# An attention and mixture-of-experts kernel: where the pieces of the product with the values stand among the nine steps of a pair

## The chip, the cores and the metric

The kernel runs on one core of a Trainium2 chip. The metric is the device time in microseconds (us) of one launch, as the median of three runs. The core's engines are called as the profile calls them: PE (TensorE, the matrix products; PEld is its loading of the stationary operand), DVE (VectorE), ACT (ScalarE), POOL (GpSimd) and SP (SyncE, which here only issues DMAs).

## The reference, cut to what matters

Eight batches of eight heads, 576 tokens, 64 values per head. Rotary embedding of q and k, softmax attention, then a mixture of eight experts with one expert for each token:

```python
q_rot, k_rot = rotate(q), rotate(k)
scores = scale * np.matmul(q_rot, k_rot.transpose(0, 1, 3, 2))
scores = scores - np.max(scores, axis=-1, keepdims=True)
attn = np.exp(scores)
attn = attn / (np.sum(attn, axis=-1, keepdims=True) + 1e-09)
x = np.matmul(attn, v)                 # 4608 tokens x 512
e_idx = np.argmax(x @ w_gate, axis=1)
...
h = np.maximum(x[mask] @ w1[e], 0.0)
out[mask] = gate_w * eom * (h @ w2[e])
```

The change touches the attention part alone.

## The kernel before, in words

Attention runs over 32 pairs (8 batches, 4 pairs of heads each). The scores of a pair are made in nine steps, numbered 0 to 8. A step makes 128 rows of scores for one head: steps 0 and 1 are the first 128 queries for head 0 and head 1, steps 2 and 3 the next 128, steps 5 and 6, and 7 and 8 likewise. Step 4 is the remainder of 64 queries for both heads at once. `Attention.step` issues, for each step in this order:

- `scores` (L473 in step 4, L480 in the others): six matrix products on PE into one of two score buffers (`ps_s`, two of them). Head 0 uses partitions 0 to 63 of its operands, head 1 uses 64 to 127, step 4 uses all 128.
- `peak` (L486): DVE takes the row maxima of the scores.
- `exp` (L495): ACT takes the exponential, which reads the score buffer for the last time. So the scores of step i+2 can't begin before the exponential of step i is over.
- events placed at this step with order 0 or 1,
- `turn` (L501): DVE turns the exponentials of the step before in 32x32 blocks,
- events with order 2 or 3.

All engines run their instructions in the order in which they were issued. What else is done in a step is listed in `EVENTS`, as (name, steps after the pair's first step, order). An offset from 9 to 17 falls into steps 0 to 8 of the next pair. The product with the values (`values`, L523) is made of 18 blocks of 32 keys. A block is eight matrix products with 32 partitions each, which the profile counts as 16 instructions. The blocks are issued in four pieces, av0 to av3, while the scores of the next pair are being made. Then follow, in order: `evict` (ACT copies the result out, L530 to L532, offset 17), `back` (PE turns it and multiplies it with the gates, L541, offset 19, that is step 1), and `divide` (DVE divides by the sums of the exponentials, L548 to L556, also step 1). The result of the next pair's pieces lies in the same PSUM tile `acc`, so av0 can't begin before `divide` of the pair before is over.

Other work of a pair that the text speaks of: ACT and POOL split the next pair's keys and queries in two parts (`kh`, `qh` at L403, `kl`, `ql` at L411), POOL multiplies and adds for the rotary embedding (L429, L433), DVE takes reciprocals of the sums (`den1`, L507), ACT moves one column (`den2`, L510).

After the fourth pair of a batch, `place` sorts the batch's tokens by expert. Its parts are spread over the following pairs, at `PLACE` (20) plus an offset, counted in steps from that fourth pair. Five of its parts (`ones`, L702, on DVE) stand at `ROWS`; five others (`places`, L709, on POOL) stand at `PLACES`. One part is a PE product (`s14`, L673 and L674, with the DVE operations L678 and L679 behind it, which need `base`, L661, from POOL) in step 1, and another is `s20` (L717, PE, with L720 on DVE behind it), also in step 1. So the pairs come in four kinds, which follow one another and are called by these parts below: the three-`ones` pair, the two-`ones` pair, the `s20` pair and the `s14` pair. The first three-`ones` pair is pair 8 (pairs are counted from 0), the last is pair 28. The second to last batch has its `ones` elsewhere.

The mixture of experts follows attention and is made of the same engines; it uses none of what is changed.

Of the kernel before, what the change touches and what calls it, by code (L numbers as in the profile page):

```python
# [44 lines left out]
EVENTS = [  # L45
# [3 lines left out]
    ("den0", 10, 2), ("den1", 12, 2), ("den2", 13, 2), ("evict", 17, 2), ("newxb", 18, 1), ("back", 19, 1), ("divide", 19, 2),  # L49
]  # L50

# [4 lines left out]
}  # L56

PIECES = ((0, 5), (5, 10), (10, 14), (14, 18))
PLACE, PM = 20, 3
LISTED = 44  # L60
ROWS, PLACES = (28, 30, 32, 37, 39), (25, 29, 31, 34, 38)

TURN = 1

# [178 lines left out]
class Attention:  # L243


    def __init__(self, tc, nb, pools, cc, ident, ii, first, trib, oneb, cnt, zero, qk, v, xd, row, lists):
# [34 lines left out]
        for n, pr in enumerate(self.pairs):  # L281
# [5 lines left out]
            for t in range(2):  # L287
# [3 lines left out]
                fs[f"loadv{t}"] = lambda pr=pr, t=t: pr.loadv(t)  # L291
            for k, (b0, b1) in enumerate(PIECES):
                fs[f"av{k}"] = lambda pr=pr, b0=b0, b1=b1: [pr.values(j) for j in range(b0, b1)]
# [950 lines left out]
```

## Time and profile before

| | |
|---|---|
| median of three runs | 1053.69 us (1051.94 to 1054.26) |
| time of the profiled execution | 1050.29 us |
| its span | 1048.4 us (the rest, 1.9 us, lies around it) |
| PE busy | 1002.2 us, 96% of the span |
| DVE busy | 819.4 us, 78% |
| ACT busy | 628.6 us, 60% |
| POOL busy | 599.5 us, 57% |
| granted PE clock, mean | 0.993 |

The profile counts a matrix product as busy from its start to its modelled end, and products overlap in it, so a PE that is shown busy may still be waiting. Where a stretch is looked at, the starts of the instructions tell more than the busy share does. The timeline view merges successive instructions of one engine, line and kind into one row, with the start, the time until the last one's end and, behind x, the count.

### The profile page before, as it was taken

The page shows a single profiled execution, that of the slowest core. Times are in us where ns is not written, and L with a number is a line of the kernel's source. Part 1 is how long each engine was busy: PE and PEld are TensorE (multiplying, and loading weights), DVE is VectorE, ACT ScalarE, POOL GpSimd, SP SyncE. Part 2 cuts the span into 40 slices and gives each one's busy share as a digit, 9 for nine tenths or more (in the row PEclk, how much of TensorE's full clock was granted, in tenths as well). Part 3 has the DMA queues.
Part 4 walks back from the last instruction along what each step waited for, and adds up shares of the span by engine and source line. Part 5 has one row for each costly group of instructions (what it writes and reads, how often), then busy time and mean ns, then how long its engine had stood idle before and what let it go on. Part 6 is the DMA issues. An engine that isn't in the chain of part 4 may idle for free.

```text
span 1048.4 us, 34822 instructions
## 1 busy us (share of the span) xinstructions
PE 1002.2 (96%) x14461; PEld 872.3 (83%) x14461; DVE 819.4 (78%) x1371; ACT 628.6 (60%) x1283; POOL 599.5 (57%) x613
## 2 busy tenths in 40 slices
PE   5999999999999999998889999999999999999995
PEld 4888888888888888887778899998889888899984
DVE  6788889898888988888777867667777867857772
ACT  4566666666666666665545444556765765857762
POOL 4777888897988879888740121305343443443621
PEclk9999999999999999999999999999999999999998
DMA  6654665565645657465457966666986977987860
GB/s 217 179 149 131 183 182 140 161 172 172 191 131 173 190 142 205 119 184 135 111 188 280 298 229 194 210 218 234 332 285 221 350 242 270 324 293 253 291 248 28
DMA packets 58209, 216.32 MB, mean 206 GB/s; under 512 B 9351, under 2 KB 9660, under 8 KB 53952
## 3 DMA queue, kind: packets, MB, share of 16 engines
q1 hardware_dynamic: 50304, 194.03, 59.4%
q0 software_dynamic: 6464, 18.92, 5.0%
q8 instruction: 115, 1.88, 0.8%
q10 hardware_dynamic: 1280, 1.11, 0.3%
q14 instruction: 46, 0.38, 0.1%
HBM read 196.04 MB, written 20.09 MB: 206 GB/s over the span
## 4 chain that ended last, share of the span: by engine, by line
PE 66%; DVE 13%; issue 7%; ACT 7%; POOL 5%; DMA 1%; ACTq 0%; POOLq 0%; DVEq 0%
PE py L1120 17%; PE ph L1078 14%; PE sc L480 13%; PE acc L523 11%; ACT pm L495 4%; PE ph L1070 4%; DVE m L486 4%; POOL raw L429 3%; DVE pt L501 2%; DVE wl L1037 2%; PE acc L541 2%; PE mtp L1043 1%; ACT kh L403 1%; ACT wh L1035 1%; DVE xb L548 1%
## 5 line engine op out<-in xcount | busy, mean ns | idle before, releaser
L495 ACT ACTIVATE pm<-sc,m 128x576 f32<-128x576 f32 x288 | 213.3, 741 | 202.7 <-DVE m L486 201.3
L1037 DVE TENSOR_TENSOR wl<-wr,wh 128x1024 fp32r<-128x1024 f32 x184 | 252.6, 1386 | 44.8 <-ACT wh L1035 42.5
L486 DVE TENSOR_REDUCE m<-sc 128x1 f32<-128x576 f32 x288 | 212.8, 739 | 67.0 <-PE sc L480 60.4
L480 PE MATMUL sc<-kh,q 64*128 64x288 f32 x1024 | 222.2, 325 | 20.3 <-ACT q L403 9.9
L501 DVE STREAM_TRANSPOSE pt<-pm 128x576 f32<-128x576 f32 x288 | 219.5, 762 | 0.3 <-ACT pm L495 0.3
L1120 PE MATMUL py<-wh,ht 128*128 128x512 f32 x640 | 215.4, 401 | 0.0
L1035 ACT CAST wh<-wr 128x1024 fp32r<-128x1024 f32 x208 | 212.6, 1050 | 0.0
L523 PE MATMUL acc<-pt,v 32*64 32x128 f32 (+1 forms) x9216 | 198.1, 296 | 9.5 <-issue 4.8
L480 PEld LDWEIGHTS sc<-kh,q 64*128 64x128 f32 x1024 | 147.2, 191 | 62.3 <-ACT pm L495 28.6
L523 PEld LDWEIGHTS acc<-pt,v 32*64 32x64 f32 x9216 | 158.4, 131 | 33.8 <-issue 25.9
L429 POOL TENSOR_TENSOR raw<-raw,rt 128x1152 f32<-128x1152 f32 x62 | 164.1, 2646 | 0.3
L1078 PE MATMUL ph<-xt,wh 128*128 128x256 f32 x896 | 161.1, 282 | 0.5 <-DVE xt L1059 0.5
L1120 PEld LDWEIGHTS py<-wh,ht 128*128 128x128 f32 x640 | 120.2, 188 | 25.7
L1078 PEld LDWEIGHTS ph<-xt,wh 128*128 128x128 f32 x896 | 138.3, 188 | 2.4 <-DVE xt L1059 1.3
L1078 PE MATMUL ph<-xt,wl 128*128 128x256 f32 x448 | 126.1, 281 | 0.0
L1120 PE MATMUL py<-wl,ht 128*128 128x512 f32 x320 | 125.9, 394 | 0.0
L480 PE MATMUL sc<-kl,q 64*128 64x288 f32 x512 | 110.6, 297 | 0.8 <-issue 0.8
L1037 POOL TENSOR_TENSOR wl<-wr,wh 128x1024 fp32r<-128x1024 f32 x24 | 58.4, 2432 | 90.2 <-ACT wh L1035 83.8
L433 POOL TENSOR_TENSOR raw<-raw 128x576 f32<-128x576 f32 x62 | 87.5, 1411 | 1.9
L1094 ACT ACTIVATE ht<-ph 128x512 fp32r<-128x512 f32 x56 | 33.4, 597 | 90.6 <-PE ph L1078 90.6
L480 PEld LDWEIGHTS sc<-kl,q 64*128 64x128 f32 x512 | 84.0, 191 | 1.1 <-issue 1.0
L1078 PEld LDWEIGHTS ph<-xt,wl 128*128 128x128 f32 x448 | 84.4, 188 | 0.1
(247 smaller groups left out, 1304.3 us busy)
## 6 DMA issues: line engine op xcount, KB each, us to landing
wr<-in_w SPq DMA_DIRECT2D x208, 512.0 KB
raw<-in_qk SPq DMA_DIRECT2D x64, 576.0 KB
v<-in_v SPq DMA_DIRECT2D x128, 288.0 KB
xd<-xb SPq DMA_DIRECT2D x16, 513.0 KB
xd<-xb SPq DMA_DIRECT2D x8, 128.2 KB
rt<-in_rope ACTq DMA_DIRECT2D x1, 576.0 KB
xg<-xd,2idx POOLq DMA_INDIRECT x18, 6.2
out<-y,2idx POOLq DMA_INDIRECT x18, 5.6
```

The costliest lines, as they stand in the source:

```text
L429: self.eng(eng).tensor_tensor(out=rv, in0=rv, in1=self.rt[:, 2 * t:2 * t + 2, x], op=ALU.mult)
L433: self.eng(eng).tensor_tensor(out=r[:, 2 * t, x], in0=r[:, 2 * t, x], in1=r[:, 2 * t + 1, x], op=ALU.add)
L480: nc.tensor.matmul(ps[:, a, :HS], self.q[r, w, c * P:c * P + P], mov[r, a * HS:a * HS + HS], start=(n == 0), stop=(n == 2))
L486: nc.vector.tensor_reduce(self.m[i], ps[:, :, :HS], axis=AX.XY, op=ALU.max, negate=True)
L495: nc.scalar.activation(pe.rearrange("p (a b) -> p a b", a=2), self.ps[i][:, :, :HS], AF.Exp, bias=self.m[i], scale=1.0, accum_out=self.z[: ...
L501: self.nc.vector.transpose(out=self.pt[:, st[0] + 5 * st[1] if st else 4, :], in_=self.pc.pop(i))
L523: nc.tensor.matmul(self.acc[h * D:h * D + D, a, o:o + 32 * n], self.v[r, h, j, :], self.pt[r, u:u + n, 32 * j:32 * j + 32], start=(j == 0) ...
L1035: self.nc.scalar.copy(wh, r)
L1037: eng.tensor_tensor(out=wl, in0=r, in1=wh.bitcast(F32), op=ALU.subtract)
L1070: nc.tensor.matmul(ph[:, 0, :], st[:, dc, 0:P], mv[:, dc, :], start=(n == 0), stop=(n == 11))
L1078: nc.tensor.matmul(ph[:, f, :], st[:, dc, fs], mv[:, dc, :], start=(n == 0), stop=(n == 11))
L1120: self.nc.tensor.matmul(py[h], st[:, f, hs], mv, start=(f == 0 and n == 0), stop=(f == 7 and n == 2))
```

## The change

Two lists of numbers change. The four pieces have 4, 5, 5 and 4 blocks in place of 5, 5, 4 and 4, and av1 and av2 stand one step earlier: the pieces stand in steps 3, 4, 6 and 8 of the next pair in place of 3, 5, 7 and 8. Three of the five `ones` on DVE move by one step: from steps 3, 5, 7, 3, 5 of their pairs to 3, 6, 8, 3, 6. Everything else is as before, and the number of instructions is the same.

```diff
     ("kl", -6, 1), ("qh", -5, 1), ("ql", -4, 1), ("lasts", 1, 2), ("loadv0", 5, 2), ("loadv1", 7, 2),
-    ("av0", 12, 1), ("av1", 14, 1), ("av2", 16, 1), ("av3", 17, 1),
+    ("av0", 12, 1), ("av1", 13, 1), ("av2", 15, 1), ("av3", 17, 1),
     ("den0", 10, 2), ("den1", 12, 2), ("den2", 13, 2), ("evict", 17, 2), ("newxb", 18, 1), ("back", 19, 1), ("divide", 19, 2),
...
-PIECES = ((0, 5), (5, 10), (10, 14), (14, 18))
+PIECES = ((0, 4), (4, 9), (9, 14), (14, 18))
 PLACE, PM = 20, 3
 LISTED = 44
-ROWS, PLACES = (28, 30, 32, 37, 39), (25, 29, 31, 34, 38)
+ROWS, PLACES = (28, 31, 33, 37, 40), (25, 29, 31, 34, 38)
```

The order of PE's work in a pair, before and after (a number is a step's scores, in brackets stands a piece with its blocks):

```
before: 0 1 back 2 3 [5] 4 5 [5] 6 7 [4] 8 [4]
after:  0 1 back 2 3 [4] 4 [5] 5 6 [5] 7 8 [4]
```

## Rows read from the trace of the kernel before

**Rows 1.** The first part of the page: of each engine the busy us, the share of the span and the instructions.

```profile
PE 1002.2 (96%) x14461; PEld 872.3 (83%) x14461; DVE 819.4 (78%) x1371; ACT 628.6 (60%) x1283; POOL 599.5 (57%) x613
```

**Rows 2.** The view that sums a stretch, here sixteen pairs in the middle of attention: its bounds, its length, the busy us of PE, PEld, DVE, ACT and POOL with their instructions, the granted PE clock, the share of the DMA engines and GB/s.

```profile
163.45:422.51 259.06, 251.94 (x5665) 212.55 (x5661) 229.22 (x445) 160.66 (x425) 221.54 (x251) 1.00 0.60 167
```

**Rows 3.** The waits of PEld and of DVE between 163.5 and 471 us: who waited for what, us in total, times, the longest.

```profile
PEld sc L480 <- ACT pm L495: 15.4, 49, 0.6
...
PEld acc L523 <- issue: 11.6, 68, 0.5
...
DVE m L486 <- PE sc L480: 33.0, 46, 1.1
```

**Rows 4.** PE's timeline from step 0 of one pair to step 0 of the next (start, us, engine, line, operation, tiles, shapes, count). L480 and L473 are scores, L523 is a piece, L541 is `back`.

```profile
350.99 0.53 PE L480 MATMUL sc<-kh,q 64*128 64x288 f32 x2
...
351.54 0.53 PE L480 MATMUL sc<-kh,q 64*128 64x288 f32 x4
...
352.52 1.63 PE L541 MATMUL acc<-ii,ac 128*128 128x160 f32 x10
354.08 0.53 PE L480 MATMUL sc<-kh,q 64*128 64x288 f32 x2
...
356.13 1.64 PE L523 MATMUL acc<-pt,v 32*64 32x160 f32 x80
357.70 0.53 PE L473 MATMUL sc<-kh,bd 128*128 128x288 f32 x2
...
358.34 0.42 PE L473 MATMUL sc<-kh,bd 128*128 128x288 f32 x2
358.88 0.53 PE L480 MATMUL sc<-kh,q 64*128 64x288 f32 x2
...
359.87 1.64 PE L523 MATMUL acc<-pt,v 32*64 32x160 f32 x80
361.44 0.53 PE L480 MATMUL sc<-kh,q 64*128 64x288 f32 x2
...
363.32 1.37 PE L523 MATMUL acc<-pt,v 32*64 32x160 f32 x64
364.62 0.53 PE L480 MATMUL sc<-kh,q 64*128 64x288 f32 x2
...
365.60 1.36 PE L523 MATMUL acc<-pt,v 32*64 32x160 f32 x64
366.90 0.53 PE L480 MATMUL sc<-kh,q 64*128 64x288 f32 x2
```

**Rows 5.** DVE's timeline in the same stretch: the maxima of steps 0 and 1, the first operation of `divide`, the maxima of steps 2 and 4, one of `ones`.

```profile
352.09 0.76 DVE L486 TENSOR_REDUCE m<-sc 128x1 f32<-128x576 f32 x1 [0.84 <-PE sc L480]
...
353.45 0.72 DVE L486 TENSOR_REDUCE m<-sc 128x1 f32<-128x576 f32 x1
...
354.77 0.66 DVE L548 TENSOR_TENSOR xb<-acc,rz 128x512 f32<-128x512 f32 x1
...
355.84 0.74 DVE L486 TENSOR_REDUCE m<-sc 128x1 f32<-128x576 f32 x1
...
358.98 0.75 DVE L486 TENSOR_REDUCE m<-sc 128x1 f32<-128x576 f32 x1
...
361.76 0.47 DVE L702 TENSOR_SCALAR_CACHE_REDUCE ro<-row,hr 128x288 fp32r<-128x288 bf16 x1
```

**Rows 6.** ACT's timeline in the same stretch: the exponentials of steps 0 to 4.

```profile
352.96 0.74 ACT L495 ACTIVATE pm<-sc,m 128x576 f32<-128x576 f32 x1 [0.69 <-DVE m L486]
...
354.27 0.74 ACT L495 ACTIVATE pm<-sc,m 128x576 f32<-128x576 f32 x1 [0.47 <-DVE m L486]
...
356.67 0.74 ACT L495 ACTIVATE pm<-sc,m 128x576 f32<-128x576 f32 x1 [1.09 <-DVE m L486]
...
358.00 0.74 ACT L495 ACTIVATE pm<-sc,m 128x576 f32<-128x576 f32 x1
...
359.82 0.74 ACT L495 ACTIVATE pm<-sc,m 128x576 f32<-128x576 f32 x1 [0.99 <-DVE m L486]
```

**Rows 7.** PE's timeline over three more pairs: `s20`, the first scores of step 4 in four pairs that follow one another, and a product of step 1 with the idle time before it.

```profile
368.43 1.12 PE L717 MATMUL acc<-ro,pl 128*128 128x288 f32 x5
...
374.53 0.53 PE L473 MATMUL sc<-kh,bd 128*128 128x288 f32 x2
...
390.43 0.53 PE L473 MATMUL sc<-kh,bd 128*128 128x288 f32 x2
...
406.18 0.53 PE L473 MATMUL sc<-kh,bd 128*128 128x288 f32 x2
...
417.43 0.40 PE L480 MATMUL sc<-kl,q 64*128 64x288 f32 x1 [0.81 <-issue]
...
422.51 0.53 PE L473 MATMUL sc<-kh,bd 128*128 128x288 f32 x2
```

**Rows 8.** POOL's timeline: `base` in a pair with `s14`, and the lower part of the queries (`ql`) in two pairs that follow one another, with POOL's idle time before it.

```profile
322.39 0.19 POOL L661 TENSOR_TENSOR base<-cnt,ct 128x8 f32<-128x8 f32 x1
...
344.98 1.42 POOL L411 TENSOR_TENSOR q<-raw,q 128x576 fp32r<-128x576 f32 x1 [0.94 <-ACT q L403]
...
361.29 1.42 POOL L411 TENSOR_TENSOR q<-raw,q 128x576 fp32r<-128x576 f32 x1 [0.91 <-ACT q L403]
```

**Rows 9.** DVE's timeline: the operation behind `s14` that needs `base`.

```profile
322.62 0.20 DVE L678 TENSOR_TENSOR pr<-acc,base 128x40 f32<-128x40 f32 x1
```

## The prediction, made before the changed kernel ran

> **What bounds the kernel now.** I read the page's first part, then the sums over a stretch of attention, the waits there, and the timelines of PE, DVE and ACT for one pair. PE is shown busy 96% of the span [rows 1] and 251.94 of 259.06 us in sixteen pairs, at granted clock 1.00, with DVE at 229.22, 88% [rows 2]. That hides waits, as the ends of products are modelled: scores waited 49 times in 19 pairs for an exponential, and DVE 33.0 us for scores [rows 3]. So neither engine bounds a pair alone. A chain does that goes through PE, DVE, ACT and back to PE, as two score buffers let the scores of step i+2 begin only after the exponential of step i.
>
> Its links are read from starts in one pair. Scores to their maximum, with DVE free: 352.09 - 350.99 = 1.10. Maximum to exponential: 352.96 - 352.09 = 0.87, or 354.27 - 353.45 = 0.82 behind a busy DVE. Exponential to the scores two steps on: 358.88 - 358.00 = 0.88. One maximum and one turn on DVE: 353.45 - 352.09 = 1.36. `divide`: 355.84 - 354.77 = 1.07 [rows 4 to 6]. On PE [rows 4]: two steps' scores in a row 1.53 (350.99 to 352.52), where the second begins 0.55 after the first, as the two use different halves of the partitions; scores alone before a piece 0.98 (364.62 to 365.60); a piece of five blocks 1.57 (359.87 to 361.44), of four 1.30 (365.60 to 366.90); `back` 1.56.
>
> These links give the pair as it is: from step 0 (350.99) to step 4 6.71, from there to the next step 0 9.20, sum 15.91 [rows 4]. In the second half step 5 waits for the exponential of step 3 (358.00 + 0.88 = 358.88, where PE alone could have begun 0.73 after step 4) and step 7 for that of step 5.
>
> **The change, step by step.** Instructions, durations and DMAs are the same; only order changes. I set the new step 4 at 0 in a pair with `ones` in step 3 and follow the links.
>
> - Exponential 3 begins at 0.45, maximum 4 at 1.43, exponential 4 at 2.26: in rows 5 and 6 they stand 0.30, 1.28 and 2.12 after step 4; 0.15 is added, since step 4 is 0.15 earlier (last point).
> - The piece of five moved from step 5 to step 4 begins at 0.98 and ends at 2.55. Step 5 begins there; its old wait (for exponential 3, over at 1.33) is hidden by the piece. Maximum 5: 3.65. DVE has been free since about 2.8, so here a new wait of DVE appears.
> - Step 6: PE is free for it at 3.10, exponential 4 lets it begin at 2.26 + 0.88 = 3.14. Piece of five (one block more than before): 4.12 to 5.69. Step 7: 5.69, its exponential (5, at 4.5) long done. That old wait goes too.
> - Maximum 6: 3.65 + 1.36 = 5.01, exponential 6: 5.83. Step 8 must wait for it: 6.71, where PE alone had 6.24. This is the new wait, 0.47. Behind it in PE's queue stand the piece av3 and the next pair's steps 0 and 1; ACT's `evict` waits for av3.
> - av3: 7.69 to 8.99. Step 0 of the next pair: 8.99, against 9.20. Maximum 7 comes at 6.84, 8 at 8.20, exponential 8 at 9.02; step 1 waits for it until 9.90, 0.36 after PE could have gone on. `back` stands behind it: 10.88.
> - The three moved `ones` take DVE about 0.47 each [rows 5]. In step 6 one stands between turn 5 and maximum 7, which then comes at 5.01 + 1.36 + 0.47 = 6.84 against 6.79 with none; in step 8 it is over before the next maximum. I cost them at nothing; the wait of DVE for scores covers them. Without that cover it would be 0.47 for each, up to 1 us per batch.
> - Maxima 0 and 1: 10.09 and 11.45. `divide` begins after a turn each side, 12.77, when `back` (10.88 + 1.63) is done; so the late `back` costs nothing. Maximum 2: 13.84, exponential 2: 14.67. Step 3: 11.45 + 0.82 + 0.88 = 13.15, av0: 14.13 to 15.43 with four blocks. Step 4 could begin at 15.43 but must wait for exponential 2: 15.55. Of the 0.27 of the block taken away 0.15 is won.
>
> So 15.55 in place of 15.91, a gain of 0.36 where `ones` stand in step 3. Without these, step 0 is at 9.03 in the old order, and the gain is 0.2.
>
> **The other kinds of pair**, from step 4 to step 4 [rows 7]. Two-`ones` to `s20` pair: 16.83 now (357.70 to 374.53). There `s20` (368.43 to 369.48, 1.05) stands between step 1 and `back`, and `divide` waits for `back`. The late step 1 now counts: `back` begins 11.93 after step 4 in place of 11.78 (369.48, the end of `s20`), so 0.15 is lost. `s20` to `s14` pair: 15.90 now (374.53 to 390.43). There DVE's operation behind `s14` begins 0.04 after POOL's `base` is over (322.39 + 0.19, then 322.62) [rows 8, 9]. POOL's chain begins at `ql`, which follows exponential 4 of that pair and isn't earlier than now. Gain 0. `s14` to three-`ones`: 15.75 now (390.43 to 406.18), to 15.53: 0.22. Three- to two-`ones`: 15.55 for 15.90 (406.18 to 422.51 is 16.33, of which 0.43 is a stop of 0.81 with no wait, partly hidden).
>
> **Sum.** 6 intervals from a three-`ones` pair (pairs 8 to 28) at 0.36: 2.2. Plain ones: pairs 1 to 4, 7, and five more `s14` ones, 10 at 0.2: 2.0. The two-`ones` pair without `s20` (pair 5): 0.3. Five to `s20`: -0.75. The `s20` pairs: 0. After pair 29 the experts' table on POOL sets the end, nothing. Together 3.8 us. The experts' part follows on PE and starts earlier by it. Against the profiled execution: 1050.29 - 3.8 = 1046.5; the median shown is 3.4 above that execution, so 1053.69 - 3.8 = 1049.9.
>
> **The unknown cost.** No row shows step 4, which uses all 128 partitions, followed by a piece at once. I took 0.98, as for the other steps. Its last two products begin at 358.34, 0.64 after its start, as they do elsewhere, and end at 358.76. Bounds: a gain is excluded, as the 0.98 is already 0.08 less than these ends allow; the worst is the whole 0.42 that those two products are shown to take. The nearest rows are step 5 before a piece (358.88 to 359.87, 0.99, lower half) and step 8 (0.98, upper half), though a piece's first loads go to the lowest partitions: so sharing the partitions or not makes 0.01. Hence 0.
>
> Here a page speaks against the change. The Trainium skill, "TensorE: Matmul & The Clock Gate", section "Part 3: Packing small matmuls — row/col tiling", says that a weight load overlaps running products only if it goes to other row groups; by that rule a piece behind step 4 has no such groups left, and the sum would be that of rival 1 below. The 0.99 and 0.98 above don't show the rule, but neither leaves a piece without any free group.
>
> **Rivals.**
> 1. *The piece behind step 4 waits for its products to end* (slower). It begins at 1.06 in place of 0.98, and the 0.17 that PEld waits ahead of a piece now (11.6 / 68 [rows 3]) comes once more behind that: 0.25 for each pair. In the 22 intervals of the sum that is 5.5, in the six `s20` to `s14` ones `base` covers all but 0.09: 6.0 in all, -3.8 + 6.0 = +2.2: 1055.9. It decides from 0.16 per pair on, where the gain is gone. For it: the page's rule named above. Against it: the equal 0.98 and 0.99. Chance 0.12.
> 2. *PE's stops with no wait* (the 0.81 of rows 7; the three- to two-`ones` intervals are about 0.5 above 15.90 on the mean of five, 2.6 us in all). In the new order the pieces of five stand closer, so the same late supply may stop PE longer. Doubled: -3.8 + 2.6 = -1.2: 1052.5, no change. Chance 0.18. If instead the new waits of steps 8 and 1 hide these stops: -6.4, 1047.3. Chance 0.12.
> 3. *POOL is next.* From `ql` to `ql` less its idle time is 16.31 - 0.91 = 15.40 [rows 8], against 15.55 new: it fits, by 0.15. If it didn't, by 0.15 or more, the three-`ones` pairs would keep half: -2.7. Also that the order on PE isn't what I wrote is a way to get nothing; the lists leave little room. Together 0.05, 1051.5.
>
> **How the numbers follow.** The forecast has 0.53, with its own range 1048.3 to 1051.5 (the links are read to 0.05, thirty times). A measurement of this kernel can tell 0.2%, 2.1 us, from no change: faster is below 1051.6, slower above 1055.8. Faster: 0.50 of the forecast, 0.12 of fewer stops, 0.04 of the rest: 0.66. Slower: 0.10 of rival 1, 0.01 else: 0.11. The same: 0.23. The range leaves out one in ten on either side: low 1046.6 (all stops gone and the links right), high 1055.0 (rival 1 short of its price, and the top of the runs shown with doubled stops).
>
> **What would show it.** Right: in the changed trace, pieces begin 0.98, 4.1 and 7.7 after step 4 in a pair with `ones`; step 5 follows the piece with no wait; PE waits about 0.5 ahead of step 8 and 0.3 ahead of step 1; three-`ones` intervals are near 15.55, those into `s20` near 16.98, `s20` to `s14` still 15.90. Wrong: a piece that begins later than 1.1 after step 4 (rival 1), more stops inside pieces or scores (rival 2), no idle time of POOL before `ql` (rival 3), or step 8 later than 6.9 after step 4, which would mean that the link from maximum 5 over DVE to exponential 6 is longer than I read.

## The result, and the profile after

The changed kernel takes 1060.51 us, median of 8 runs (1058.20 to 1066.88), the kernel before 1052.47 us in its 8 (1050.30 to 1055.40). The ratio is 1.0085, with a 95% interval of 1.0057 to 1.0113: slower, by 8.0 us in the medians, where 3.8 us less were forecast. The profiled execution took 1061.71 us, its span is 1059.8 us.

The first lines are the page's: busy time by engine, and the two groups of the pieces (L523), with their idle time before and what ended most of it. The last two are the same groups on the page of the kernel before.

```profile
PE 1004.7 (95%) x14461; PEld 873.5 (82%) x14461; DVE 817.9 (77%) x1371; ACT 628.2 (59%) x1283; POOL 601.2 (57%) x613
...
L523 PE MATMUL acc<-pt,v 32*64 32x128 f32 (+1 forms) x9216 | 206.7, 302 | 19.7 <-issue 14.9
...
L523 PEld LDWEIGHTS acc<-pt,v 32*64 32x64 f32 x9216 | 163.9, 134 | 45.2 <-issue 37.4
```

```profile
L523 PE MATMUL acc<-pt,v 32*64 32x128 f32 (+1 forms) x9216 | 198.1, 296 | 9.5 <-issue 4.8
...
L523 PEld LDWEIGHTS acc<-pt,v 32*64 32x64 f32 x9216 | 158.4, 131 | 33.8 <-issue 25.9
```

The busy shares have hardly moved from [rows 1]. The pieces have: before, PE stood idle 9.5 us ahead of them, 4.8 of these with no wait that the profile shows ("issue"), and PEld 33.8 us, 25.9 of them "issue". Now it is 19.7 and 14.9, and 45.2 and 37.4.

The sixteen pairs of [rows 2] in the sums over a stretch, now 266.36 us long in place of 259.06, and the waits that answer to [rows 3], again between 163.5 and 471 us:

```profile
166.23:432.59 266.36, 253.37 (x5661) 213.26 (x5661) 228.78 (x445) 160.75 (x425) 221.87 (x253) 0.98 0.58 163
```

```profile
PEld acc L523 <- issue: 17.9, 71, 2.2
...
PEld sc L480 <- ACT pm L495: 11.5, 36, 0.5
PEld sc L473 <- ACT pm L495: 8.0, 19, 0.5
```

```profile
DVE m L486 <- PE sc L480: 39.4, 44, 3.6
```

The granted PE clock is 0.98 where it was 1.00. PEld's waits for an exponential ahead of L480 have shrunk from 15.4 to 11.5 us, those ahead of step 4 (L473) have grown from 4.0 to 8.0; the forecast had both, as the old waits of steps 5 and 7 go and step 4 now waits for exponential 2. The idle time ahead of pieces that no wait explains has grown from 11.6 us in 68 to 17.9 in 71, and the longest is 2.2 us in place of 0.5.

**Where the time went.** The start of step 4 (L473 in PE's timeline) marks off the pairs, as in [rows 7]. The table sums the intervals between these starts, worked out from the timelines of the two profiled executions, by the kind of pair in which they begin:

```
intervals from                  before    after   difference
pairs 1 to 5 (no ones, no s20)   78.53    80.32       +1.79
three-ones pairs, six           101.22   111.12       +9.90
two-ones pairs, six             101.17   102.46       +1.29
s20 pairs, six                   95.38    95.32       -0.06
s14 pairs, six                   94.52    93.32       -1.20
pair 30                          19.54    19.54        0.00
```

Together that is 11.7. Step 4 of pair 1 begins 1.0 earlier than before (35.41 in place of 36.41), so that of the last pair comes 10.7 us later, of 11.4 us between the two executions. The three-`ones` pairs make nearly all of it. One by one they took 16.87, 16.70, 15.91, 16.32, 16.33 and 19.10 us before and 19.11, 18.65, 16.74, 19.97, 16.84 and 19.82 after.

**A pair that runs as forecast.** PE's timeline from step 4 of an `s14` pair to step 4 of the next:

```profile
199.28 0.53 PE L473 MATMUL sc<-kh,bd 128*128 128x288 f32 x2 [0.19 <-ACT pm L495]
...
200.26 1.64 PE L523 MATMUL acc<-pt,v 32*64 32x160 f32 x80
201.83 0.53 PE L480 MATMUL sc<-kh,q 64*128 64x288 f32 x2
...
203.19 1.64 PE L523 MATMUL acc<-pt,v 32*64 32x160 f32 x80
204.76 0.53 PE L480 MATMUL sc<-kh,q 64*128 64x288 f32 x2
...
205.98 0.53 PE L480 MATMUL sc<-kh,q 64*128 64x288 f32 x2 [0.16 <-ACT pm L495]
...
206.97 1.37 PE L523 MATMUL acc<-pt,v 32*64 32x160 f32 x64
208.26 0.53 PE L480 MATMUL sc<-kh,q 64*128 64x288 f32 x2
...
209.92 1.63 PE L541 MATMUL acc<-ii,ac 128*128 128x160 f32 x10
...
214.82 0.54 PE L473 MATMUL sc<-kh,bd 128*128 128x288 f32 x2
```

From 199.28 on: piece at 0.98, step 5 at 2.55 with no wait, piece at 3.91, step 7 at 5.48, step 8 at 6.70 after a wait for an exponential, piece at 7.69, step 0 at 8.98, `back` at 10.64, next step 4 at 15.54. The forecast had 0.98, 2.55, 4.12 with `ones` in step 3, 5.69, 6.71, 7.69, 8.99, 10.88 and 15.53. Six of the nine are there to 0.03 us. The 4.12 and 5.69 hold where `ones` stand in step 3: here piece and step 7 come 0.21 earlier, and in the three-`ones` pair below the piece begins at 4.13. `back` comes 0.24 earlier than forecast.

**A pair that doesn't.** The same view for the first three-`ones` pair:

```profile
147.13 0.53 PE L473 MATMUL sc<-kh,bd 128*128 128x288 f32 x2
...
148.12 1.64 PE L523 MATMUL acc<-pt,v 32*64 32x160 f32 x80
...
151.26 1.58 PE L523 MATMUL acc<-pt,v 32*64 32x160 f32 x73
155.06 0.50 PE L523 MATMUL acc<-pt,v 32*64 32x128 f32 x7 [2.22 <-issue]
...
157.39 2.36 PE L523 MATMUL acc<-pt,v 32*64 32x160 f32 x64
159.67 0.53 PE L480 MATMUL sc<-kh,q 64*128 64x288 f32 x2
...
166.23 0.53 PE L473 MATMUL sc<-kh,bd 128*128 128x288 f32 x2
```

The piece in step 6 begins on time (151.26), issues 73 of its 80 counted instructions and then stands still until 155.06, in the middle of its blocks, where it has nothing to wait for. Then the next piece, of four blocks, takes 2.36 us in place of 1.37. The stretch view in steps of 2 us (columns as in rows 2) shows why:

```profile
151.00:153.00 2.00, 1.84 (x76) 1.38 (x74) 2.00 (x4) 0.87 (x3) 2.00 (x2) 1.00 0.71 233
153.00:155.00 2.00, 0.00 (x0) 0.00 (x0) 0.95 (x3) 0.79 (x2) 2.00 (x2) 1.00 0.77 185
155.00:157.00 2.00, 1.94 (x18) 1.72 (x19) 0.19 (x1) 0.00 (x0) 2.00 (x3) 0.78 0.96 289
157.00:159.00 2.00, 2.00 (x54) 1.72 (x61) 2.00 (x4) 0.84 (x3) 2.00 (x2) 0.50 0.51 190
159.00:161.00 2.00, 2.00 (x34) 1.51 (x25) 1.22 (x4) 1.72 (x5) 2.00 (x3) 0.87 0.16 34
161.00:163.00 2.00, 2.00 (x14) 1.79 (x14) 2.00 (x4) 0.89 (x3) 1.03 (x2) 1.00 1.03 263
```

From 153 to 155 PE issued nothing. After that the granted clock is 0.78 and then 0.50, that is 1.2 GHz in place of 2.4, and it is back at 1.00 from 161 on. So a stop of 2.2 us cost this interval 19.11 - 15.55 = 3.6 us. Of the six three-`ones` intervals after, the four of 18.65 us and more have a stretch at 0.50 behind their stop, 20.5 us in all; those of 16.74 and 16.84 have a stop and no such stretch. The six stops alone, from start to start, sum to 10.9 us.

SP's timeline shows what the DMA engines had to move at that time, and the DMA view counts the packets of each queue that began in a stretch, first 145.2 to 152.6 us, then 152.6 to 152.8:

```profile
145.16 0.40 SPq L656 DMA_DIRECT2D xd<-xb  x1
145.60 1.32 SPq L424 DMA_DIRECT2D v<-in_v  x2
146.97 0.42 SPq L656 DMA_DIRECT2D xd<-xb  x1
152.31 0.35 SPq L417 DMA_DIRECT2D raw<-in_qk  x1
```

```profile
q1 hardware_dynamic: 629, 1.62, 83.3%
```

```profile
q8 instruction: 1, 0.02, 34.0%
q1 hardware_dynamic: 9, 0.01, 16.2%
```

Two stores of x (513 KB each) leave in this pair, with two loads of v between them. For 7.4 us the engines work for these and no packet of q8 begins. At 152.6, as this burst ends, one does: 16 KB of instructions (0.02 MB). q8 moved 115 packets in the whole execution, and PE has 14461 products and as many loads: 251 of them for each packet. 2.3 us after that short stretch PE goes on. The kernel before shows the same in the same pair on a smaller scale: the stores leave at 144.41 and 146.23, a q8 packet begins between 151.5 and 151.7, where that burst ends, and 2.3 us later, at 154.01, a piece goes on that had stopped for 0.52 us:

```profile
q8 instruction: 1, 0.02, 33.9%
```

```profile
154.01 0.52 PE L523 MATMUL acc<-pt,v 32*64 32x128 f32 x13 [0.52 <-issue]
```

**Where in PE's order it stops.** The stretch view and the DMA view, both of the changed kernel, from the start of the span to 154 us, in the stop above, and to 221.5 us, in the stop of the next three-`ones` pair:

```profile
0.00:154.00 154.00, 137.69 (x2779) 115.98 (x2779) 124.75 (x218) 91.87 (x234) 112.62 (x113) 1.00 0.60 169
0.00:221.50 221.50, 201.13 (x4185) 169.34 (x4185) 181.82 (x328) 132.20 (x340) 167.92 (x176) 0.99 0.59 167
```

```profile
q8 instruction: 21, 0.34, 0.9%
q8 instruction: 32, 0.52, 1.0%
```

From the one stop to the other PE has begun 1406 products and as many loads. With four semaphore instructions of PE, which the view leaves out, these are 2816, that is 11 times 256, and q8 has begun 11 packets. The same holds in all thirteen traces of this document: in pairs 1 to 29 there are 41 gaps of more than 1.0 us in which PE begins no product and no load. Each comes when PE has begun 193 plus a multiple of 256 instructions, and the multiple is the number of packets that q8 has begun before PE goes on. PE goes on 2.2 to 3.3 us after the last of these began. So what was fetched was used up, and the next 256 instructions, one packet, came late. The stop in [rows 7] (0.81 us idle, 1.10 from start to start) is one of the 41.

The same count tells what the new order changed. Take, in each three-`ones` pair, the packet at which the changed kernel stops. It begins 2.3 to 4.1 us after PE has begun the last 256 instructions ahead of it. The same packets, by their numbers, begin 2.0 to 3.8 us after that place in the kernel before, and without the stores (e3 below) from 0.4 us ahead of it to 1.0 us after it. Where nothing stops PE, it gets through these 256 instructions in 3.7 to 4.9 us in the new order (e3) and in 4.0 to 6.2 us in the old one (e13). So the packet is about as late as it was, and PE needs it sooner.

### The profile page after: what moved, and what is told of

Read it like the earlier page. It is cut to its first block, busy times and chain, and to the rows that moved or that the text cites. A ratio compares the mean times of both kernels' runs of the same rounds, so it can differ in the third digit from the quotient of the medians.

```text
span 1059.8 us, 34822 instructions
## 1 busy us (share of the span) xinstructions
PE 1004.7 (95%) x14461; PEld 873.5 (82%) x14461; DVE 817.9 (77%) x1371; ACT 628.2 (59%) x1283; POOL 601.2 (57%) x613
## 4 chain that ended last, share of the span: by engine, by line
PE 63%; DVE 15%; issue 9%; ACT 5%; POOL 5%; DMA 2%; ACTq 0%; POOLq 0%; DVEq 0%
PE py L1120 17%; PE ph L1078 14%; PE sc L480 11%; PE acc L523 10%; DVE m L486 5%; PE ph L1070 4%; DVE pt L501 4%; ACT pm L495 4%; PE sc L473 3%; POOL raw L429 2%; DVE wl L1037 2%; PE acc L541 1%; PE mtp L1043 1%; DVE xb L548 1%; ACT wh L1035 1%
## 5 line engine op out<-in xcount | busy, mean ns | idle before, releaser
L1037 DVE TENSOR_TENSOR wl<-wr,wh 128x1024 fp32r<-128x1024 f32 x184 | 251.8, 1382 | 45.2 <-ACT wh L1035 42.6
L480 PE MATMUL sc<-kh,q 64*128 64x288 f32 x1024 | 218.9, 330 | 16.4 <-ACT q L403 9.4
L523 PE MATMUL acc<-pt,v 32*64 32x128 f32 (+1 forms) x9216 | 206.7, 302 | 19.7 <-issue 14.9
L523 PEld LDWEIGHTS acc<-pt,v 32*64 32x64 f32 x9216 | 163.9, 134 | 45.2 <-issue 37.4
L480 PEld LDWEIGHTS sc<-kh,q 64*128 64x128 f32 x1024 | 151.8, 194 | 56.8 <-ACT pm L495 23.1
L480 PE MATMUL sc<-kl,q 64*128 64x288 f32 x512 | 111.1, 301 | 0.0
L480 PEld LDWEIGHTS sc<-kl,q 64*128 64x128 f32 x512 | 85.6, 195 | 0.0
```

The costliest lines, as they stand in the source:

```text
L480: nc.tensor.matmul(ps[:, a, :HS], self.q[r, w, c * P:c * P + P], mov[r, a * HS:a * HS + HS], start=(n == 0), stop=(n == 2))
L523: nc.tensor.matmul(self.acc[h * D:h * D + D, a, o:o + 32 * n], self.v[r, h, j, :], self.pt[r, u:u + n, 32 * j:32 * j + 32], start=(j == 0) ...
L1037: eng.tensor_tensor(out=wl, in0=r, in1=wh.bitcast(F32), op=ALU.subtract)
```

## The experiments

Theory S: PE's next instructions are fetched by DMA in pieces of 16 KB; in a three-`ones` pair that fetch is served only when the burst of loads and stores is over; the changed order has issued fourteen of eighteen blocks by then and runs dry, and the stop then costs clock too. The intervals in this table are worked out from the starts of step 4 in each profiled execution, as above (three-`ones`: the six one by one; two-`ones`: their sum; plain: the median of the `s14` ones). The text calls a run by the first part of its name.

```
run                    median  ratio [95%]              three-ones                          two-ones  plain
changed               1060.51  1.0085 [1.0057,1.0113]   19.11 18.65 16.74 19.97 16.84 19.82   102.46  15.55
e1_rows_back          1069.31  1.0139 [1.0071,1.0206]   20.81 21.19 18.66 20.44 18.79 20.36   102.54  15.56
e3_no_stores          1050.79  0.9981 [0.9958,1.0004]   15.57 15.55 15.56 15.56 15.55 15.57   102.64  15.56
e4_shift128           1069.79  1.0138 [1.0083,1.0193]   21.10 21.07 21.26 16.92 20.48 17.46   101.79  15.56
e5_steps_alone        1066.77  1.0136 [1.0088,1.0184]   19.41 19.72 16.68 17.06 18.06 18.58   103.25  15.70
e6_sizes_alone        1059.16  1.0051 [1.0032,1.0071]   16.48 16.81 16.17 17.18 19.90 17.82   103.84  15.86
e8_stores_spread      1050.88  0.9979 [0.9957,1.0000]   15.56 15.56 15.56 15.55 15.56 15.56   107.53  15.55
e10_gap_stores        1047.97  0.9935 [0.9910,0.9961]   15.56 15.55 15.57 15.56 15.58 15.55   106.37  15.55
e12_gap_stores_all    1044.22  0.9957 [0.9942,0.9973]   15.56 15.55 15.56 15.56 15.55 15.58   104.03  15.55
e11_before_gap_stores 1045.03  0.9915 [0.9883,0.9946]   16.05 15.91 15.90 15.88 15.89 15.91   101.00  15.77
e13_before_gap_again  1043.54  0.9951 [0.9932,0.9970]   15.90 15.90 15.91 15.90 15.89 15.88   101.19  15.75
e14_before_more       1059.63  1.0102 [1.0071,1.0134]   21.94 22.96 15.92 16.19 16.76 19.33   102.01  15.76
before                   -        -                     16.87 16.70 15.91 16.32 16.33 19.10   101.17  15.75
```

Ratios are to the kernel before on the same chip, whose median was 1052.47 us for the changed kernel, 1053.8 us for e1 to e11 and 1049.05 us for e12 to e14. So ratios compare, medians of different rows only roughly.

**The moved `ones`** (the changed kernel with the old places):

```diff
-ROWS, PLACES = (28, 31, 33, 37, 40), (25, 29, 31, 34, 38)
+ROWS, PLACES = (28, 30, 32, 37, 39), (25, 29, 31, 34, 38)
```

> The changed kernel with the `ones` of DVE put back to their old steps (3, 5, 7, 3, 5); the pieces stay in steps 3, 4, 6 and 8. Theory S (PE runs out of instructions in the three-`ones` pairs, because the fetch of its next 16 KB stands behind the stores of x that leave in these pairs): no change, 1058 to 1062 us, three-`ones` intervals still 16.7 to 20. Rival O (the moved `ones` delay a maximum and with it PE): back near 1050 us.

1069.31 us, and the three-`ones` intervals are no shorter. Rival O falls. The time is above the range given; the plain intervals are the same, all of it lies in the three-`ones` ones, 120.25 us in place of 111.12. Their six stops sum to 13.1 us in place of 10.9, and the granted clock is 0.50 for 37.5 us in place of 20.5. Why the stops are longer isn't shown.

**No stores** (the changed kernel without the stores of x of six batches):

```diff
-        fs += [(25, 2, s13), (31, 2, lambda: store(0)), (33, 2, lambda: store(1)), (34, 2, lambda: store(2)), (37, 2, no)]
+        fs += [(25, 2, s13)]
...
-                out=self.xgs[s % 2][:, h, :], out_offset=None, in_=self.xd[0:n, :],
+                out=self.xgs[s % 2][:, h, :], out_offset=None, in_=self.w.rearrange("r c -> (r c)")[0:n * XW].rearrange("(n d) -> n d", d=XW),
```

> The changed kernel without the stores of x for the first six batches (the gather of the tokens reads the weights instead, so the experts work on other data; the time of the gathers is the same). Theory S: all six three-`ones` intervals fall to about 15.55 us and the time falls by 17.8 us, to 1041 to 1046 us. Rival O, or a rival by which PE's stops come from the closer pieces alone (D): the intervals stay at 16.7 and more and the time within 3 us of the changed kernel's.

Step 4 of the first three-`ones` pair and the next step 4, in PE's timeline:

```profile
146.58 0.54 PE L473 MATMUL sc<-kh,bd 128*128 128x288 f32 x2
...
162.15 0.53 PE L473 MATMUL sc<-kh,bd 128*128 128x288 f32 x2
```

15.57 in place of 19.11, and so in all six: 93.35 us in place of 111.12. Without the stores these pairs have no stops. D falls: the closer pieces alone don't stop PE here. The total fell by less than forecast. The interval of pair 30, where the gather begins, is 25.66 us long in place of 19.54; that this comes with the other data of the gather is likely and not shown.

**Chunk ends moved** by 64 transposes, that is 128 PE instructions, ahead of the first scores:

```diff
+    dummy = small.tile("dummy")
+    for _ in range(64):
+        nc.tensor.transpose(out=dummy[:, 0, :], in_=ident, identity=ident)
     att.start(consts)
```

> The changed kernel with 64 idle transposes (128 PE instructions) ahead of the first scores, which moves the places in PE's order at which a 16 KB chunk ends by half a chunk. Theory S with density (fourteen of eighteen blocks within seven us need the chunk in time wherever its end lies): the six three-`ones` intervals stay at 16.7 to 20, 1057 to 1063 us. Rival A (bad luck in where the chunks end): they change by 2 us and more each, and the time could be 1046 to 1053 us.

The sum stays high (118.29 us) and all six pairs still stop, so the order isn't just unlucky. The time, 1069.79 us, is above both ranges, and each interval changed by about 2 us or more, as A had it: the fourth went from 19.97 to 16.92, the third from 16.74 to 21.26. How much of that comes from where a chunk ends, and how much differs from one execution to the next, isn't shown by one trace of each.

**Steps alone, sizes alone**: the changed kernel with the old sizes, and the kernel before with the new ones:

```diff
-PIECES = ((0, 4), (4, 9), (9, 14), (14, 18))
+PIECES = ((0, 5), (5, 10), (10, 14), (14, 18))
```

and

```diff
-PIECES = ((0, 5), (5, 10), (10, 14), (14, 18))
+PIECES = ((0, 4), (4, 9), (9, 14), (14, 18))
```

> The changed kernel with the old sizes of the pieces: 5, 5, 4 and 4 blocks in steps 3, 4, 6 and 8. Theory S (PE's next 16 KB of instructions come only when the burst of loads and stores in a three-`ones` pair is over, and PE runs dry if it has issued too many blocks by then): fourteen blocks are again issued before step 7, so the three-`ones` intervals stay at 17 to 21 us and the time at 1056 to 1070 us. Rival Z (it is the sizes that cost, a piece of five in step 6): three-`ones` intervals of 16 to 17 us and 1048 to 1053 us.

> The kernel before with the sizes 4, 5, 5 and 4 in the old steps 3, 5, 7 and 8. Theory S: only nine blocks are issued before step 6, one fewer than in the kernel before, so the three-`ones` intervals are 15.8 to 17.5 us, the time 1050 to 1056 us. Rival Z: three-`ones` intervals of 17 us and more, 1056 us and more.

The steps bring the stops: 109.51 us in the six, as S has it, with one of 16.68 below its range, and Z falls as the whole cause. The sizes alone cost something too, 1.0051 and 1059.16 us, above what S had and within what Z had: their six are 104.36 us with two of 19.90 and 17.82, and in the old steps they make even the pairs without stops longer, 15.86 in place of 15.75, 16.03 in place of 15.90 from `s20` pairs and some 17.2 in place of 16.83 into them. The 0.2 us of a plain interval need steps and sizes together: steps alone give 0.05.

**Stores spread**, each behind a load of v:

```diff
-        fs += [(25, 2, s13), (31, 2, lambda: store(0)), (33, 2, lambda: store(1)), (34, 2, lambda: store(2)), (37, 2, no)]
+        fs += [(25, 2, s13), (33, 2, lambda: store(0)), (42, 2, lambda: store(1)), (43, 2, lambda: store(2)), (37, 2, no)]
```

> The changed kernel with the three stores of x of a batch issued one by one: the first after the second load of v in the three-`ones` pair (it stood between the two), the second after that of the pair behind, the third at the start of the pair after that. Each burst of DMA is then at most 1.1 MB in place of 1.6 MB. Theory S: the fetch is no longer late by much, three-`ones` intervals 15.6 to 16.5, 1044 to 1050 us, below the kernel before. Rivals O and D: within 3 us of the changed kernel's 1060 us.

The three-`ones` intervals are all at 15.56, as forecast, but the total only came down to that of the kernel before. The stop has moved with the store: the two-`ones` intervals sum to 107.53 us. In PE's timeline, the first two-`ones` pair (161.70 to 181.97, 20.27 us) has it now. The DMA view of 163.3 to 163.5 has the packet, 2.3 us ahead of the piece that goes on at 165.82:

```profile
161.70 0.53 PE L473 MATMUL sc<-kh,bd 128*128 128x288 f32 x2
...
165.82 0.52 PE L523 MATMUL acc<-pt,v 32*64 32x160 f32 x12 [1.56 <-issue]
...
181.97 0.53 PE L473 MATMUL sc<-kh,bd 128*128 128x288 f32 x2 [0.20 <-ACT pm L495]
```

```profile
q8 instruction: 1, 0.02, 35.0%
```

**Stores in the gaps**, with both orders. The second store is issued by ACT in step 3 of the two-`ones` pair, where the DMA engines were quiet:

```diff
-    def store(i):
+    def store(i, eng=nc.sync):
...
-            nc.sync.dma_start(out=xd[r:r + 2 * P, :].rearrange("(c p) d -> p c d", p=P), in_=xbs[b][:, 2 * i:2 * i + 2, 0:XW])
+            eng.dma_start(out=xd[r:r + 2 * P, :].rearrange("(c p) d -> p c d", p=P), in_=xbs[b][:, 2 * i:2 * i + 2, 0:XW])
...
-        fs += [(25, 2, s13), (31, 2, lambda: store(0)), (33, 2, lambda: store(1)), (34, 2, lambda: store(2)), (37, 2, no)]
+        fs += [(25, 2, s13), (33, 2, lambda: store(0)), (37, 2, lambda: store(1, nc.scalar)), (42, 2, lambda: store(2))]
```

> The changed kernel with its stores of x where the DMA is quiet: the first behind both loads of v in the three-`ones` pair (as in the run with spread stores, where its intervals were 15.56 us), the second issued by ACT in step 3 of the two-`ones` pair, between its loads of v and of the next q and k, the third (128 KB) at that pair's end. Theory S: three-`ones` intervals 15.56, two-`ones` ones near 16.95 with at most 1 us of stops, the time 1044 to 1049 us, 2 to 6 us under the run with spread stores. If the fetch is late for other reasons: stops of 1 to 3 us stay in two-`ones` intervals, 1050 us and more.

> The kernel before with the same new places of the stores. Theory S: its three-`ones` intervals fall to 15.9 (from a mean of 16.9), the time by some 5 us, to 1046 to 1050 us; the kernel with the changed order and the same stores is 2 to 4 us below it, which is the gain that the links forecast (0.36 in each three-`ones` interval, 0.2 in plain ones). If the forecast's links are wrong too: no difference between the two, or this one below.

> The old order with the stores of x in the gaps once more, in more rounds: 1042 to 1048 us, a ratio of 0.990 to 0.995 to the kernel before. If the first run of it was luck: a ratio within 0.997 to 1.003.

The old order now has no stops: step 4 to step 4 of its first three-`ones` pair is 15.90 us, and the idle time ahead of pieces between 163.5 and 471 us has no entry over 0.2 (start of the two step 4; PEld's waits):

```profile
145.66 0.53 PE L473 MATMUL sc<-kh,bd 128*128 128x288 f32 x2
...
161.56 0.53 PE L473 MATMUL sc<-kh,bd 128*128 128x288 f32 x2
```

```profile
PEld acc L523 <- issue: 10.9, 67, 0.2
```

Its ratio is 0.9915 and, in more rounds, 0.9951 [0.9932, 0.9970]: the stores' places were worth some 5 us in the kernel before, without any change to the pieces. The changed order came from 1.0085 to 0.9935 by it, its time in the range forecast, but stops stayed in two-`ones` pairs (106.37, one of them 19.02) and in pairs 1 and 2 (17.23 and 19.73 us), which have no stores; the longest of these, 1.9 us in pair 2, lies at the end of a chunk as the others do. The forecast that it would be 2 to 4 us below the old order failed.

> The changed order with the first store as in the run before, and the second and the third both issued by ACT in step 3 of the two-`ones` pair, so that the burst of q, k and v ahead of them is 128 KB shorter. Theory S: the stops in the two-`ones` intervals shrink (sum of the six from 106.4 to 102 to 105 us), those in pairs 1 and 2, where no stores are, stay; 1043 to 1048 us. A rival by which the stops in two-`ones` pairs come from the store that ACT issues: they stay or grow, 1048 us and more.

```diff
...
-        fs += [(25, 2, s13), (31, 2, lambda: store(0)), (33, 2, lambda: store(1)), (34, 2, lambda: store(2)), (37, 2, no)]
+        fs += [(25, 2, s13), (33, 2, lambda: store(0)), (37, 2, lambda: (store(1, nc.scalar), store(2, nc.scalar)))]
```

104.03 us in the two-`ones` pairs, as S had it, and 0.9957 [0.9942, 0.9973], which is level with the old order's 0.9951. Its gains, 2.0 us in three-`ones` intervals and 1.2 in the `s14` ones against e13, are given back in two-`ones` pairs (2.8, of which the order itself takes some 0.1 each, 16.94 for 16.83) and in pair 1 (1.2, with a stop of 0.9).

**More traffic in the old order** (513 KB more in each three-`ones` pair):

```diff
+    global EXTRA
+    EXTRA = dpool.tile([NT, XW], F32, name="xd2")
...
+        if i == 1:
+            nc.sync.dma_start(out=EXTRA[r:r + 2 * P, :].rearrange("(c p) d -> p c d", p=P), in_=xbs[b][:, 2 * i:2 * i + 2, 0:XW])
```

> The kernel before with one store more in every three-`ones` pair: the second one (513 KB) is written twice, once to memory that nobody reads. Theory S by dose: the fetch of instructions comes later by the time of these 513 KB, some 2 us, so the old order too runs dry: three-`ones` intervals rise from a mean of 16.9 to 18 to 20.5 us, the others stay at 16.83, 15.90 and 15.75; 1058 to 1075 us. If DMA traffic isn't the cause: unchanged, 1050 to 1056 us.

Half met. The time rose by 10 us to 1.0102, and the plain intervals and those behind didn't change. But only two of the six three-`ones` pairs took the blow, 21.94 and 22.96 us; the other four stayed within 0.5 of what they were. In these two the packet begins 4.5 and 4.0 us after PE has begun the 256 instructions ahead, which PE gets through in 4.1 and 4.0 us where nothing stops it (e13), and the stops are 3.0 and 3.2 us. In the other four it begins 1.9 to 4.0 us after, PE takes 4.6 to 6.2 us there, and no stop over 0.2 us stands at that place. The first pair, in steps of the stretch view, shows stop and clock as in the changed kernel:

```profile
153.00:155.00 2.00, 0.00 (x0) 0.00 (x0) 0.83 (x3) 0.83 (x2) 2.00 (x3) 1.00 0.90 235
155.00:157.00 2.00, 1.53 (x16) 1.10 (x17) 0.00 (x0) 0.00 (x0) 2.00 (x2) 0.58 1.00 350
157.00:159.00 2.00, 2.00 (x41) 1.72 (x47) 0.93 (x2) 0.08 (x1) 2.00 (x3) 0.50 0.23 87
```

## Why the prediction was wrong

- *What bounds a pair, and the links.* Right. Step 5 without a wait, the new wait ahead of step 8, most starts to 0.03 us (`back` came 0.24 earlier), 15.55 in a plain interval (15.53), 15.56 in three-`ones` ones where nothing disturbs them (15.55), 15.88 from `s20` pairs (15.90), 16.94 into them where they run free (16.98).
- *The unknown cost, rival 1.* The piece behind step 4 begins 0.98 to 1.00 after it in pairs 2 to 30, so the 0 that was taken for it was right. The rule on row groups that was weighed there, from the Trainium skill, "TensorE: Matmul & The Clock Gate", section "Part 3: Packing small matmuls — row/col tiling", by which it would have cost more, doesn't show in this case.
- *The moved `ones` at nothing.* Nothing speaks against it: with the old places (e1) the plain intervals are the same and the three-`ones` ones no shorter.
- *The step that failed: "Instructions, durations and DMAs are the same; only order changes".* Same instructions don't mean the same supply of instructions. The stop of 0.81 us with no wait was read, and set down as rival 2 with 2.6 us in all, which might double; chance 0.18. What was not asked is what such a stop is. The SP and DMA views would have told: most stops stand in pairs with stores, and a q8 packet comes as the burst ends. From that, the question would have been how soon the new order uses up what PE has: it issues fourteen blocks before step 7, where the old order had ten before step 6 and fourteen only before step 8, and so 256 instructions go in 3.7 to 4.9 us in place of 4.0 to 6.2. The 2.6 us also left out the sixth three-`ones` interval, 19.10. The stops in three-`ones` intervals grew from 101.22 - 95.39 = 5.8 us (95.39: the six of e13) to 111.12 - 93.35 = 17.8 us, threefold.
- *What a stop costs.* It was priced at what it added to an interval of the kernel before, 0.43 us for a stop of 0.81, and at most doubled. A stop of 2.2 us was followed by a granted clock of 0.50 (157 to 159 us) and cost 3.6 us.
- *The gain of 3.8 us* shows in part: 2.0 us in three-`ones` intervals and 1.2 in `s14` ones, e12 against e13. No run shows it in the whole time (0.9957 and 0.9951). Even with the stores out of the way the new order stopped in pair 1 and in two-`ones` pairs.
- *Rival 3, POOL,* didn't come up: three-`ones` intervals reached 15.56.

That PE runs out of fetched instructions is shown by the 41 stops, and that the stores' traffic makes the packet late by e3, where it is on time, and by e8 and e14, which move the traffic and find the stop moved. What stays open is where the time is lost. The trace has the start of the packet, not of its request, so that it *waits* for the burst's end is argued. Why the stops of e1 are longer than those of the changed kernel stays open too, and the traffic behind the stops in pairs 1 and 2 was not changed by any run.

## What to carry to other kernels

Before instructions on a busy engine are packed closer, look for idle time that the profile puts down to "issue" in the middle of a run of products, and lay SP's timeline and the instruction queue's packets beside it: a loop may already be living on the gaps between DMA bursts. Counting PE's instructions from one such stop to the next tells whether it is the fetch: here they were 11 times 256. A burst is then part of the engine's path although none of its data is waited for, and moving a store to a quiet stretch can be worth more than the reordering (here 0.9951 with the old order untouched). A stop on PE also has to be priced with the clock that follows it (here 3.6 us for a stop of 2.2).

## What the runs showed of the hardware that was not expected

A fetch of 16 KB of instructions began only at the end of a burst of 7.4 us, and PE stood for 2.2 us although none of its operands was late. The Trainium skill, "Runtime: NRT & Kernel Launch", section "Instruction fetch mechanics", says that instructions are refilled in blocks of 16 KiB, which agrees with the packets here (115 of 0.02 MB), and that the cost of crossing a block's end is mostly hidden; in this case it is not, and the measurement decides. The Trainium skill, "DMA: Bandwidth & Descriptors", section "Queues, rings and completion order", says that a DMA engine goes round its queues packet by packet; by that a fetch would get its turn within a burst. In the stretch above no packet of q8 began in 7.4 us of traffic of q1, 3.95 us of them after PE had begun the last 256 instructions that it had, where the packet begins up to 1.0 us after that without the stores. If it was asked for as early as there, the trace doesn't bear the rule out; the request itself isn't in it.
